# Who copies the key rows of the second score operand: VectorE or GpSimd

## The chip, the cores and the metric

The kernel runs on one core of a Trainium2 chip. The core has a matrix engine (TensorE, PE in the rows, with a queue of its own for weight loads, PEld), a vector engine (VectorE, DVE), a scalar engine (ScalarE, ACT), a general one (GpSimd, POOL) and a queue that issues the transfers (SyncE, SP). The metric is the device time of one execution in microseconds, as the median of several runs. The times of single instructions come from one further execution that was profiled.

## The reference

An attention with a forgetting bias for 8 batches of 8 heads, 576 positions and 64 values a head, and behind it a channel mix of width 512 and 1024:

```
scores = q @ k.T / sqrt(64)
cum = cumsum(max(s, 0))
bias = -(cum[query] - cum[key])
scores = where(causal, -1e9, scores + min(bias, 0))
attn = softmax(scores)
x = attn @ v                              # heads side by side: 8 x 576 x 512
xk = mu_k * x + (1 - mu_k) * x_prev       # x_prev: the position before
xr = mu_r * x + (1 - mu_r) * x_prev
out = sigmoid(xr @ w_r) * (max(xk @ w_k, 0) ** 2 @ w_v)
```

## The kernel before

Every product that must be exact to float32 is split in high and low halves: an operand x becomes xh (x rounded to the matrix engine's format fp32r) and xl = x - xh, and the product is a sum of two or three matmuls.

For the scores of a head (`scores`, matmuls at line 761) there are two passes. The first multiplies G (the rounded queries, both halves of the partitions alike) with KH. KH holds the rounded keys on 64 partitions and their low part on the other 64. The second pass multiplies QL (the low part of the queries on 64 partitions, and three rows of ones) with KL. KL holds the keys on 64 partitions and, below them, three rows with the running sums of s, which bring the bias. The first four visits (the early part of the first batch) use a plain form without these halves.

`split_qk` makes these operands for two heads at a time (j is 0 or 1), from the raw keys k and the raw queries, which lie in buffers called raw: the three rows of sums by a transfer (line 687), ScalarE's copy of the keys into K, which is KH's high half (line 693), GpSimd's subtraction for KH's low half (line 697), VectorE's cast of the keys into KL (line 703), ScalarE's copy of the queries into G (line 708), and GpSimd's subtraction for QL (line 712). It is called 32 times, for 64 heads. KL, QL, G and KH have three buffers each and raw four.

Other names that the prediction uses: line 779 is VectorE's masking of the scores with the running minimum nm; line 797 ScalarE's exponents into W; lines 834 and 839 the sum and its reciprocal rinv (GpSimd, then VectorE); line 813 GpSimd's normalisation of W, five pieces to a head; line 856 the transposes of W on TensorE into the bank t; lines 885 and 889 ph (ScalarE's rounding of the transposed weights) and pl (VectorE's low part); lines 1005 and 1019 the matmuls with V into po; line 632 V's low part on GpSimd, after ScalarE's copy at line 628; lines 1123, 1130, 1152 and 1156 the mixing of neighbouring positions and its halves xh and xl; lines 1184, 1226 and 1251 the matmuls of the channel mix, which works on 18 chunks of 256 positions; line 608 the low half of a weight.

The order of the instructions on every engine is made by a planner in the kernel, the class `Plan`, before the program is built. Each step is added with its engine, an assumed duration and what it reads and writes. The planner lets all engines run by these assumptions, forward and backward in turns, and keeps the best of 20 orders. The functions pe, act, dve, pool and dma add a step to an engine; two of them are:

```python
def dve(emit, reads, writes, n, rate=0.96, extra=70, quarters=(0, 0)):
    return at_quarters(plan.add("DVE", n / rate + extra, emit, reads, writes), quarters)
...
def pool(emit, reads, writes, n, extra, rate=0.8333, quarters=(0, 0)):
    return at_quarters(plan.add("POOL", n * rate + extra, emit, reads, writes), quarters)
```

quarters says on which quarters of the partitions a step reads and writes; the planner puts a gap of 20 ns where they change from a step to the next on an engine. Each engine works through its part of the order strictly in sequence.

Of the kernel before, what the change touches and what calls it, by code (L numbers as in the profile page):

```python
# [29 lines left out]
def f32(ap):  # L30
    return ap.bitcast(F32)
# [281 lines left out]
def forgetting_attention_then_channel_mix(  # L313
# [16 lines left out]
    nc = tc.nc  # L330
# [22 lines left out]
    def sbuf(shape, tag, bufs=1, dtype=F32):  # L353
        return plan.buffer(sb, shape, dtype, tag, bufs)
# [15 lines left out]
    def at_quarters(i, quarters):  # L370
        if quarters != (0, 0):
            plan.quarters[i] = quarters
        return i

    def act(emit, reads, writes, n, extra=51, table=0, quarters=(0, 0)):
        return at_quarters(
            plan.add("ACT", n * 0.8333 + extra, emit, reads, writes, land=table), quarters
# [8 lines that stand above are left out]
    def dma(emit, reads, writes, ns):  # L386
        return plan.add("SP", 1.286 * ns, emit, reads, writes, land=1300)
# [279 lines left out]
    def ahead(emit, what, n):  # L667
        due, plan.due = plan.due, -2.0e5
        dve(emit, [], [what], n)
        plan.due = due  # L670

    def split_qk(b, hp, qs, k):

        nq, nk = qs[0].n, k.n
        found = []
        for j in range(2):
            own, other = slice(64 * j, 64 * j + 64), slice(64 - 64 * j, P - 64 * j)  # L680
            QQ, K = (sbuf([P, n], x, 3, F32R) for n, x in ((nq, "G"), (nk, "KH")))
            QL, KB = (sbuf([P, S], x, 3, F32R) for x in ("QL", "KL"))
            if made[0] < 3:
                made[0] += 1
                ahead(lambda QL=QL: nc.vector.memset(f32(QL.get()[64:67]), 1.0), (QL, 1), S)
            dma(
                lambda j=j, KB=KB: nc.sync.dma_start(
                    f32(KB.get()[64:67, 0:nk]), cum3_d.ap[b * H + 2 * hp + j, :, 0:nk]
                ),
                [(cum3_d, i) for i in range(3)], [(KB, 1)], 40,  # L690
            )
            act(
                lambda own=own, K=K: nc.scalar.copy(K.get()[own], k.get()[own]),  # L693
                [(k, j)], [(K, j)], nk, 90,
            )
            pool(
                lambda own=own, other=other, K=K: nc.gpsimd.tensor_tensor(  # L697
                    out=K.get()[other], in0=k.get()[own], in1=f32(K.get()[own]), op=ALU.subtract
                ),
                [(k, j), (K, j)], [(K, 1 - j)], nk, 210, 2.21, (2 * j, 2 - 2 * j),  # L700
            )
            dve(
                lambda own=own, KB=KB: nc.vector.tensor_copy(KB.get()[0:64, 0:nk], k.get()[own]),  # L703
                [(k, j)], [(KB, 0)], nk, 1.92, 150, (2 * j, 0),
            )
            x = qs[j]
            act(
                lambda x=x, QQ=QQ: nc.scalar.copy(QQ.get(), x.get()),  # L708
                [(x, 0), (x, 1)], [(QQ, 0), (QQ, 1)], nq, 90,
            )  # L710
            pool(
                lambda x=x, QQ=QQ, QL=QL: nc.gpsimd.tensor_tensor(  # L712
                    out=QL.get()[0:64, 0:nq], in0=x.get()[0:64], in1=f32(QQ.get()[0:64]),
                    op=ALU.subtract,
                ),
                [(x, 0), (QQ, 0)], [(QL, 0)], nq, 210, 2.21,
            )
            found.append(((QQ, K, P), (QL, KB, 67)))
        return found
# [632 lines left out]
    def prepare(n):  # L1352
        qs, ks = loaded.pop(n)
        b, hp, tiles = visits[n]
        vn = load_values(b, hp, -(-KN[tiles[-1]] // P), n < PLAIN)
        QKs[n] = [[(x, ks)] for x in qs] if n < PLAINQ else split_qk(b, hp, qs, ks)
        Vs[n] = vn if n < PLAIN else split_v(vn, vn.n // P)
# [119 lines left out]
```

## Time and profile before

| | |
|---|---|
| median of 3 runs | 872.01 us (871.11 to 875.14) |
| the profiled execution | 871.47 us, of it span of the instructions 869.7 us |
| TensorE matmuls busy | 851.7 us, 98% of the span |
| TensorE weight loads busy | 751.0 us, 86% |
| VectorE busy | 698.5 us, 80% |
| ScalarE busy | 688.4 us, 79% |
| GpSimd busy | 449.5 us, 52% |
| granted TensorE clock | 0.999 of full speed |

Busy times are the sum of an engine's instructions without overlaps. Matmuls follow each other in a pipeline, each counted from its start to its modelled end, so a busy TensorE can still be one that starts its matmuls late. The span runs from the first to the last instruction.

### The profile page before, as it was taken

Reading aid. Unit: us, or ns where it says so; the run is one execution under the profiler, and the core shown is the slowest. Engines: PE = TensorE matmul, PEld = TensorE weight load, DVE = VectorE, ACT = ScalarE, POOL = GpSimd, SP = SyncE. Lnnn points to the kernel's source line nnn. Section 1 sums busy time; section 2 is a strip of 40 time slices with the busy share of each in tenths; the row PEclk is TensorE's granted clock in tenths of the full one; section 3 lists DMA queues with packets and bytes.
Section 4 is the critical chain, followed back from the end, with each engine's and each line's share of the span. In section 5 each row is a group of like instructions: output and inputs, shape, how many; then the busy total and the mean of one; then the engine's idle time right before and its main releaser. Section 6 shows DMA issues by size and latency. Waiting matters only on the chain.

```text
span 869.7 us, 17512 instructions
## 1 busy us (share of the span) xinstructions
PE 851.7 (98%) x5519; PEld 751.0 (86%) x5519; DVE 698.5 (80%) x2143; ACT 688.4 (79%) x1854; POOL 449.5 (52%) x719
## 2 busy tenths in 40 slices
PE   9999999999999999999999999999999999999998
PEld 8778789789888888989898988898988889888986
DVE  8999789889888998789878888888888888555431
ACT  6999999999978987898979787988887978445331
POOL 5877887884754665455646545445653642000000
PEclk9999999999999999999999999999999999999999
DMA  8775233251332323223322313132412110100100
GB/s 248 254 233 154 86 115 109 85 153 47 109 117 67 120 64 110 67 83 93 89 88 72 109 55 120 58 104 72 122 55 92 44 62 16 57 22 34 49 25 24
DMA packets 48125, 80.10 MB, mean 92 GB/s; under 512 B 8160, under 2 KB 21472, under 8 KB 48032
## 3 DMA queue, kind: packets, MB, share of 16 engines
q1 hardware_dynamic: 48032, 78.99, 29.7%
q8 instruction: 43, 0.70, 0.3%
q14 instruction: 50, 0.41, 0.2%
HBM read 59.64 MB, written 19.33 MB: 91 GB/s over the span
## 4 chain that ended last, share of the span: by engine, by line
PE 76%; DVE 12%; ACT 8%; issue 3%; DMA 1%; SPq 0%; POOL 0%; ACTq 0%; DVEq 0%
PE m L1251 16%; PE m L1184 16%; PE m L1226 9%; PE s L761 8%; PE po L1019 7%; PE t L856 7%; DVE W L779 3%; ACT W L797 3%; DVE KL L703 2%; DVE pl L889 2%; PE t L1251 2%; PE po L1005 2%; PE s L1184 2%; PE t L1184 2%; PE s L750 1%
## 5 line engine op out<-in xcount | busy, mean ns | idle before, releaser
L1184 PE MATMUL m<-xh,w_k 128*128 128x256 f32 x976 | 205.5, 288 | 0.5 <-ACT xh L1152 0.3
L797 ACT ACTIVATE W<-W,nm 64x64 f32<-64x64 f32 (+4 forms) x320 | 179.6, 562 | 26.3 <-DVE nm L779 22.0
L1251 PE MATMUL m<-w_v,kh 128*128 128x512 f32 x528 | 187.6, 406 | 0.0
L813 POOL TENSOR_SCALAR W<-W,rinv 128x192 f32<-128x192 f32 (+4 forms) x320 | 166.7, 540 | 25.4 <-DVE rinv L839 23.8
L1184 PEld LDWEIGHTS m<-xh,w_k 128*128 128x128 f32 x976 | 160.2, 189 | 3.0 <-ACT xh L1152 0.7
L779 DVE CUSTOM_DVE_ANT_0 W<-s,lower 128x448 f32<-128x448 f32 (+5 forms) x320 | 130.1, 414 | 26.2 <-PE s L761 21.0
L1184 PE MATMUL m<-xl,w_k 128*128 128x256 f32 x488 | 138.9, 285 | 0.0
L856 PE MATMUL t<-ident,W 128*128 128x128 f32 (+1 forms) x736 | 134.0, 275 | 4.5 <-DVE xT L1057 1.8
L697 POOL TENSOR_TENSOR KH<-raw,KH 64x576 fp32r<-64x576 f32 x64 | 92.9, 1451 | 83.9 <-ACT KH L693 45.5
L889 DVE TENSOR_TENSOR pl<-t,ph 128x512 fp32r<-128x512 f32 x224 | 106.4, 484 | 11.9 <-ACT ph L885 9.9
L856 PEld LDWEIGHTS t<-ident,W 128*128 128x128 f32 (+1 forms) x736 | 89.5, 137 | 25.7 <-DVE xT L1057 2.8
L1251 PEld LDWEIGHTS m<-w_v,kh 128*128 128x128 f32 x528 | 97.9, 189 | 14.3 <-ACT g L1238 0.3
L761 PE MATMUL s<-KH,G 128*64 128x64 f32 (+1 forms) x360 | 108.7, 309 | 0.5 <-DVE nm L779 0.5
L885 ACT CAST ph<-t 128x512 fp32r<-128x512 f32 x224 | 93.2, 424 | 17.4 <-PE t L856 14.6
L761 PE MATMUL s<-KL,QL 67*64 67x64 f32 (+1 forms) x360 | 106.1, 299 | 0.0
L1251 PE MATMUL m<-w_v,kl 128*128 128x512 f32 x264 | 106.0, 402 | 0.0
L1130 DVE SCALAR_TENSOR_TENSOR xp<-x,mu,xp 128x256 f32<-128x256 f32 (+3 forms) x184 | 76.3, 415 | 26.5 <-ACT xp L1123 24.1
L1226 PE MATMUL m<-w_r,xh 128*128 128x512 f32 x264 | 95.1, 406 | 0.5 <-DVE kl L1213 0.5
L1123 ACT ACTIVATE xp<-x,mu 128x256 f32<-128x256 f32 (+3 forms) x184 | 77.6, 422 | 22.3 <-DMA x<-x_d 11.7
L712 POOL TENSOR_TENSOR QL<-raw,G 64x576 fp32r<-64x576 f32 (+1 forms) x64 | 86.6, 1353 | 13.3 <-ACT G L708 11.2
L1184 PEld LDWEIGHTS m<-xl,w_k 128*128 128x128 f32 x488 | 92.4, 189 | 0.9
L632 POOL TENSOR_TENSOR V<-vn,V 128x320 fp32r<-128x320 f32 x56 | 48.4, 882 | 70.9 <-ACT V L628 64.5
(161 smaller groups left out, 1899.6 us busy)
## 6 DMA issues: line engine op xcount, KB each, us to landing
raw<-in_q SPq DMA_DIRECT2D x112, 144.0 KB
raw<-in_k SPq DMA_DIRECT2D x32, 288.0 KB
out<-g SPq DMA_DIRECT2D x36, 256.0 KB
vn<-in_v SPq DMA_DIRECT2D x28, 320.0 KB
x_d<-xT SPq DMA_DIRECT2D x28, 288.5 KB
x<-x_d SPq DMA_DIRECT2D x11, 514.0 KB
w_k<-in_moe_w_k SPq DMA_DIRECT2D x8, 512.0 KB
w_v<-in_moe_w_v SPq DMA_DIRECT2D x8, 512.0 KB
```

What stands on the lines that cost most here:

```text
L697: lambda own=own, other=other, K=K: nc.gpsimd.tensor_tensor(out=K.get()[other], in0=k.get()[own], in1=f32(K.get()[own]), op=ALU.subtract),
L712: lambda x=x, QQ=QQ, QL=QL: nc.gpsimd.tensor_tensor(out=QL.get()[0:64, 0:nq], in0=x.get()[0:64], in1=f32(QQ.get()[0:64]), op=ALU.subtract,),
L761: lambda x=x, G=G, K=K, n=n: nc.tensor.matmul(ps.get()[:m, :w], G.get()[:n, q0 : q0 + m], K.get()[:n, k0 : k0 + w], start=x == 0, stop=x == 1,
L779: lambda a=a, e=e, to=to, i=i: nc.vector.tensor_tensor_reduce(out=W.ap[:m, to : to + e - a], in0=ps.get()[:m, a - k0 : e - k0], in1=lower. ...
L797: lambda: nc.scalar.activation(W.ap[:m, :n], W.ap[:m, :n], AF.Exp, bias=nm.get()[:m, 3 * t + mi : 3 * t + mi + 1], scale=-1.0, accum_out=s ...
L813: lambda: nc.gpsimd.tensor_scalar(out=to.ap[:m, c : c + n], in0=W.ap[:m, :n], scalar1=rinv.get()[:m, t : t + 1], scalar2=1.0, op0=ALU.mult ...
L856: lambda: nc.tensor.transpose(ps.get()[0:m, place : place + P], pt[t].ap[:, k0 + front(t, tiles) : k0 + front(t, tiles) + m], ident.ap,),
L885: act(lambda: nc.scalar.copy(strips(ph), src()), [ps], [(ph, k) for k in ks], n * m)
L889: lambda: nc.vector.tensor_tensor(out=strips(pl), in0=src(), in1=f32(strips(ph)), op=ALU.subtract),
L1184: lambda u=u, f=f, c=c, n=n, w=w, x=x: nc.tensor.matmul(ps.get()[:, u * CT : (u + 1) * CT], weight["k", c, f // 4].get()[:, w, f % 4 * P : ...
L1226: lambda c=c, n=n, x=x, w=w: nc.tensor.matmul(ps.get(), x.get()[:, c, ts], weight["r", c, 0].get()[:, w], start=c == 0 and n == 0, stop=c ...
L1251: lambda f=f, n=n, x=x, w=w: nc.tensor.matmul(ps.get(), x.get()[:, f, ts], weight["v", f, 0].get()[:, w], start=f == 0 and n == 0, stop=f ...
```

## The change

The cast of the keys into KL moves from VectorE to GpSimd, with the duration that the planner assumes for GpSimd (576 x 0.8333 + 244). ScalarE's copy of the keys is given the quarters of the partitions on which it works, which no instruction uses, only the planner.

```diff
             act(
                 lambda own=own, K=K: nc.scalar.copy(K.get()[own], k.get()[own]),
-                [(k, j)], [(K, j)], nk, 90,
+                [(k, j)], [(K, j)], nk, 90, quarters=(2 * j, 2 * j),
             )
...
-            dve(
-                lambda own=own, KB=KB: nc.vector.tensor_copy(KB.get()[0:64, 0:nk], k.get()[own]),
-                [(k, j)], [(KB, 0)], nk, 1.92, 150, (2 * j, 0),
+            pool(
+                lambda own=own, KB=KB: nc.gpsimd.tensor_copy(KB.get()[0:64, 0:nk], k.get()[own]),
+                [(k, j)], [(KB, 0)], nk, 244, 0.8333, (2 * j, 0),
             )
```

Both edits change what the planner sees, and it writes a new order for all engines. Two places show what becomes of the instructions. In these rows a name before the arrow is written and those behind it are read; the numbers in the names are those of buffers and differ between the two programs.

The first place is on VectorE, around the 61st of the 64 casts, where VectorE changes from the scores of one head to those of the next (line 779 writes W_72, then W_71). Before, it reads:

```order
L889 TENSOR_TENSOR pl<-t_310,ph_1439 128x512
L779 ISA W_72,nm_254<-s_146,lower,nm_254 128x64
L779 ISA nm_254 128x1
L779 ISA W_71,nm_229<-s_143,lower 64x64
L779 ISA nm_229 64x1
L703 CAST KL_569<-raw_357 64x576
L1156 TENSOR_TENSOR xl_897<-xp_307,xh_882 128x512
L889 TENSOR_TENSOR pl<-t_316,ph_1439 128x384
L889 TENSOR_TENSOR pl<-t_310,ph_1439 128x256
L839 RECIPROCAL rinv_313<-rinv_313 128x5
```

Of the change, VectorE's order has at the same change of heads:

```order
L889 TENSOR_TENSOR pl<-t_291,ph_1416 128x512
L779 ISA W_72,nm_213<-s_151,lower,nm_213 128x64
L779 ISA nm_213 128x1
L779 ISA W_71,nm_181<-s_149,lower 64x64
L779 ISA nm_181 64x1
L889 TENSOR_TENSOR pl<-t_291,ph_1416 128x256
L889 TENSOR_TENSOR pl<-t_296,ph_1416 128x384
L839 RECIPROCAL rinv_271<-rinv_271 128x5
```

The cast is gone, the subtraction for xl stands ten rows ahead of the first of these, and the two pieces of pl have changed places.

The second place is on GpSimd, in the preparation of the pair of heads to which that cast belongs. Before, it reads:

```order
L632 TENSOR_TENSOR V_1411<-vn_100,V_1411 128x5x64 x2
L697 TENSOR_TENSOR KH_524<-raw_357,KH_524 64x576
L1415 MEMSET xT_201 128x1
L712 TENSOR_TENSOR QL_110<-raw_433,G_439 64x576
L834 TENSOR_SCALAR rinv_313<-sums_157 128x5
L726 MEMSET sums_157 128x1
L813 TENSOR_SCALAR W_72<-W_72,rinv_313 128x192
L813 TENSOR_SCALAR W_72<-W_72,rinv_313 128x320
L813 TENSOR_SCALAR W_72<-W_72,rinv_313 128x448
L813 TENSOR_SCALAR W_72<-W_72,rinv_313 64x64
L813 TENSOR_SCALAR W_72<-W_72,rinv_313 128x576
```

Of the change, the same pair of heads reads:

```order
L703 CAST KL_552<-raw_299 64x576
L712 TENSOR_TENSOR QL_109<-raw_381,G_366 64x576
L697 TENSOR_TENSOR KH_468<-raw_299,KH_468 64x576
L632 TENSOR_TENSOR V_1401<-vn_92,V_1401 128x5x64
L834 TENSOR_SCALAR rinv_271<-sums_157 128x5
L632 TENSOR_TENSOR V_1401<-vn_92,V_1401 128x5x64
L813 TENSOR_SCALAR W_72<-W_72,rinv_271 128x192
L813 TENSOR_SCALAR W_72<-W_72,rinv_271 128x320
L813 TENSOR_SCALAR W_72<-W_72,rinv_271 128x448
L813 TENSOR_SCALAR W_72<-W_72,rinv_271 64x64
L813 TENSOR_SCALAR W_72<-W_72,rinv_271 128x576
```

The cast of the head's keys stands ahead of its subtractions, QL's has moved ahead of KH's, and V's two pieces come after them, with the sum of line 834 between. The five normalisations of line 813 keep their places at the end.

## Rows read from the trace of the kernel before

**Rows 1.** Windows: stretch in us, its length, busy us of each engine (instructions), clock, transfers
```profile
0.00:240.00 240.00, 230.46 (x1531) 199.31 (x1532) 218.25 (x638) 221.62 (x618) 184.19 (x298) 1.00 0.47 144
240.00:700.00 460.00, 455.25 (x2986) 405.15 (x2984) 390.43 (x1295) 387.67 (x1055) 252.40 (x394) 1.00 0.28 85
700.00:870.00 170.00, 165.97 (x1005) 146.50 (x1005) 89.86 (x212) 79.11 (x183) 12.91 (x27) 0.99 0.11 37
```
**Rows 2.** The chain that ended last, its shares of the span by engine and line
```profile
by line: PE m L1251 16.2%; PE m L1184 16.1%; PE m L1226 9.4%; PE s L761 8.0%; PE po L1019 6.9%; PE t L856 6.6%; issue 2.7%; DVE W L779 2.6%; ACT W L797 2.6%; DVE KL L703 2.3%; DVE pl L889 2.0%; PE t L1251 1.9%; PE po L1005 1.9%; PE s L1184 
```
**Rows 3.** Line 703: its group (busy us, mean ns, idle before); its durations, shortest, median, longest
```profile
L703 DVE CAST KL<-raw 64x576 fp32r<-64x576 f32 x64 | 50.1, 784 | 1.0
L703 DVE CAST KL<-raw x64: 417/518/2062, 33.5 to 698.3; 64x576 fp32r<-64x576 f32 x64
```
**Rows 4.** Windows of line 703 alone, in the first and the middle stretch
```profile
0.00:240.00 240.00, 20.89 (x26) 1.00 0.47 144
240.00:700.00 460.00, 29.26 (x38) 1.00 0.28 85
```
**Rows 5.** Timeline from 659 to 663 us: start, length, instruction [idle before, releaser]
```profile
659.42 1.43 POOL L712 TENSOR_TENSOR QL<-raw,G 64x576 fp32r<-64x576 f32 x1 [0.57 <-ACT G L708]
...
659.60 1.56 DVE L703 CAST KL<-raw 64x576 fp32r<-64x576 f32 x1
...
661.69 0.87 DVE L889 TENSOR_TENSOR pl<-t,ph 128x384 fp32r<-128x384 f32 x2
...
662.28 0.42 PE L1019 MATMUL po<-pl,V 128*64 128x448 f32 x1 [0.85 <-DVE pl L889]
...
662.75 0.43 POOL L813 TENSOR_SCALAR W<-W,rinv 128x192 f32<-128x192 f32 x1 [1.33 <-DVE rinv L839]
```
**Rows 6.** Timeline from 243.7 to 248 us
```profile
244.02 1.42 POOL L712 TENSOR_TENSOR QL<-raw,G 64x576 fp32r<-64x576 f32 x1 [0.64 <-ACT G L708]
...
244.10 2.06 DVE L703 CAST KL<-raw 64x576 fp32r<-64x576 f32 x1
...
246.67 0.42 PE L1019 MATMUL po<-pl,V 128*64 128x448 f32 x1 [0.81 <-DVE pl L889]
```
**Rows 7.** Waits of TensorE's load queue: us in total, times, longest
```profile
PEld po L1019 <- DVE pl L889: 7.2, 12, 1.3
PEld po L1005 <- ACT ph L885: 3.3, 5, 1.0
PEld t L856 <- DVE xT L1057: 2.8, 4, 0.8
PEld t L856 <- ACT ph L922: 2.5, 6, 0.7
PEld t L856 <- DVE pl L889: 2.4, 11, 0.4
PEld s L761 <- DVE nm L779: 2.0, 6, 0.9
PEld t L856 <- DVE pl L943: 1.7, 2, 0.9
PEld t L1019 <- DVE pl L889: 1.3, 2, 0.7
```
**Rows 8.** Groups on GpSimd that are nearest to the new cast; the fill by its durations
```profile
L697 POOL TENSOR_TENSOR KH<-raw,KH 64x576 fp32r<-64x576 f32 x64 | 92.9, 1451 | 83.9 <-ACT KH L693 45.5 <-PE m L1184 9.0 <-PE s L761 7.9
L813 POOL TENSOR_SCALAR W<-W,rinv 128x576 f32<-128x576 f32 x64 | 48.1, 752 | 0.0
...
L465 POOL MEMSET raw<- x1: 577/577/577, 0.9 to 0.9; 64x576 f32 x1
```
**Rows 9.** Line 1156 on VectorE by its durations
```profile
L1156 DVE TENSOR_TENSOR xl<-xp,xh x72: 640/687/694, 48.7 to 832.8; 128x512 fp32r<-128x512 f32 x72
```
**Rows 10.** Waits of GpSimd
```profile
POOL rinv L834 <- ACT W L797: 70.4, 32, 13.5
POOL V L632 <- ACT V L628: 64.5, 17, 9.5
```

## The prediction

> **What bounds the kernel now.** I read the busy time by stretches first [rows 1]. The program has three stretches: up to 240 us everything runs at once (weight splitting, attention, the first chunks), from 240 to 700 us attention and channel mix alternate, and after 700 us little but channel mix is left. TensorE is busy nearly all the time in each, but its matmuls overlap, so that share says little of how often it waited. The telling numbers are those of its feeders: in the first stretch VectorE is busy 218.25 of 240 us (91%) and ScalarE 221.62 (92%), GpSimd 184.19 (77%); in the middle one VectorE has 390.43 of 460 us (85%), ScalarE 387.67 (84%), GpSimd 252.40 (55%). So VectorE and ScalarE run level just behind TensorE, and GpSimd has room, least of it early.
>
> Next the chain of work that ended last [rows 2]: mostly matmul lines, but the key cast at line 703 alone carries 2.3% of 869.7 us, 20.0 us. That is a lot for 64 instructions. Their own row [rows 3] says why: shortest 417 ns, median 518, mean 784, longest 2062. Something stretches them.
>
> The timeline shows what. At 659.42 us GpSimd starts a 1.43 us subtraction for QL; at 659.60 VectorE starts the cast, which takes 1.56 us, ending 0.31 us after the subtraction. Behind it in VectorE's order, as shown above, stand xl (line 1156) and pl (line 889), which starts at 661.69; the matmul on pl starts at 662.28 after TensorE has stood 0.85 us, "released by pl", and the normalisation on GpSimd (line 813) waits 1.33 us for its reciprocal, which is queued behind pl [rows 5]. At 244.10 us it is the same with 2.06 us of cast and 0.81 us of standing TensorE [rows 6]. Other VectorE work is not stretched so: the 72 subtractions of line 1156 lie between 640 and 694 ns [rows 9].
>
> Last the waits of TensorE's weight-load queue [rows 7]: the six rows that VectorE ends sum to 7.2 + 2.8 + 2.4 + 2.0 + 1.7 + 1.3 = 17.4 us. This and the chain's 20.0 us are two upper views of what VectorE costs TensorE today.
>
> **The change part by part.**
>
> *Removed from VectorE*: 64 casts, 50.1 us [rows 3], of it 20.89 us in the first stretch and 29.26 us in the middle [rows 4]. Taken at the shortest, 64 x 417 ns = 26.7 us is copying; the other 23.4 us is stretching. VectorE falls to 197.4 of 240 us (82%) and 361.2 of 460 us (79%). What reaches TensorE: in the two places looked at, 0.85 + 0.81 = 1.66 us of standing matmuls for 1.56 + 2.06 = 3.62 us of cast, 46% [rows 5, 6]. Lower bound 0 (all waits are taken over by other work), upper bound the 20.0 us of the chain. I take 46% of the 20.0 us: 9.2 us, which is about half of the 17.4 us of visible waits.
>
> *Added to GpSimd*: 64 casts of 64x576. No such row exists. The nearest below is the fill of a tile of the same shape, 577 ns; the nearest above the subtraction with two inputs and the same shape, 1451 ns; between them the one-input multiply of 128x576, 752 ns [rows 8]. One input and one output make it most like the last: 752 ns, 48.1 us in all. In the first stretch that is 26 x 0.752 = 19.6 us, GpSimd 203.8 of 240 us (85%); in the middle 38 x 0.752 = 28.6 us, 281 of 460 us (61%). In the middle it has cover: it stood idle 83.9 us ahead of the KH subtraction (45.5 us of that for ScalarE's K copy) [rows 8], 64.5 us ahead of V's subtraction and 70.4 us ahead of the sum of line 834 [rows 10], and the new cast stands ahead of that KH subtraction in the order. Without cover, queued behind it on GpSimd are the KH and QL subtractions, and then the five normalisations of a head, for which the transposes of line 856 wait. Lower bound of the harm 0, upper bound the 19.6 us of the crowded first stretch. I charge 1 us, close to the lower end, since 55.8 us of that stretch are idle on GpSimd.
>
> *The wait moves with the cast.* It needs the raw keys alone, which the subtraction on the same queue needs too, so no new transfer is waited for. The raw keys had three readers on three engines (ScalarE's copy, the subtraction, the cast) and now have two of them on GpSimd; I cost that at nothing because a reader on GpSimd, the subtraction, already held the buffer before, and 207.6 us of the middle stretch are idle there [rows 1] to cover a later release. Without that cover the next load into raw would come late by one cast, 752 ns.
>
> *The quarters given to ScalarE's copy* add no instruction; they and the moved task only change what the planner assumes. It then writes another order for every engine. The orders shown above are alike in kind (VectorE's loses the cast row, the rest keeps its sequence but for neighbours), so I count this at zero, with 4 us to either side for the luck of a new order.
>
> Sum: 871.47 (the profiled execution) - 9.2 + 1 = 863.3, say 863.5 us. The profiled execution lies 0.5 us below the median 872.01 of the runs, so nothing is added for that. It is 1.0% faster.
>
> One rule speaks against it. The Trainium skill, "Perfetto Trace Analysis", section "Optimizing Scalar/DVE Operations", warns that moving work between VectorE and GpSimd might not help, because they share a pair of SBUF ports which a two-port VectorE instruction holds alone. The trace agrees with the sharing, and shows it from the other side: the cast was stretched to 1.56 us by a GpSimd instruction [rows 5]. By that rule the sum would be 871.5; it is the third rival. I go by the rows, since they show one VectorE line that is stretched, and it is the one that leaves.
>
> **The rivals.**
>
> 1. *All of the chain's share comes back* (VectorE no longer late anywhere, also for the reciprocal and the normalisation behind it): 871.5 - 20.0 = 851.5 us. For it: the casts' delay is unplanned, and the order is static, so each delay travels on. Against it: in both places other VectorE work stood between the cast and pl, and TensorE lost under half.
>
> 2. *ScalarE takes over*. It is already the busier one in the first stretch [rows 1], and TensorE's load queue waits for it too, 3.3 us and 2.5 us in two rows beside those counted above [rows 7]. If VectorE is early and ScalarE late, a quarter of the 9.2 us may be left: 871.5 - 2.3 + 1 = 870.2 us.
>
> 3. *The two engines go on hindering each other*, now with GpSimd's cast: the time saved on VectorE is lost in its other instructions, 871.5 us. Against it stand the narrow times of line 1156 [rows 9].
>
> 4. *Slower: GpSimd becomes late in the first stretch.* If a cast there cost as much as the two-input subtraction, 1.451 us, 26 of them are 37.7 us, and GpSimd stands at 221.9 of 240 us, as full as ScalarE. The normalisations then come late by a cast, and with the same 46% reaching TensorE that costs 26 x 1.451 x 0.46 = 17.4 us, against a gain in the middle stretch of 9.2 x 29.26/50.15 = 5.4 us: 871.5 + 17.4 - 5.4 = 883.5 us. It decides from a cast of about (221.6 - 184.2)/26 = 1.44 us on. For it: GpSimd is at 77% there before the change. Against it: the one-input row is half of that.
>
> **How the numbers follow.** My forecast has 0.60 (863.5, itself 859 to 867 by the 4 us of the order), the whole share 0.08 (851.5), ScalarE 0.15 (870.2), mutual hindrance 0.05 (871.5), slower 0.12 (883.5). A measurement of this kernel tells about 0.5%, 4.4 us, from no change, so faster is below 867.6: 0.60 + 0.08 = 0.68; same 0.15 + 0.05 = 0.20; slower 0.12. The range leaves out the slower rival and most of the first: 854 to 871.5 us.
>
> **What would show it.** Right: line 703 stands on GpSimd at 0.65 to 0.9 us with hardly any scatter; VectorE's total falls by about 50 us; the chain holds next to nothing of line 703; the load queue's waits that VectorE ends fall from 17.4 to about half; GpSimd's busy time rises by about 48 us, and it releases few TensorE waits. Wrong: new waits of line 856 for line 813 in the first 240 us (rival 4), waits for ScalarE's ph, V or exponents of the size of those that went (rival 2), VectorE lines longer than before (rival 3), or a start or an end of the program that the new order moved, which none of these terms holds.

## The result, and the profile after

| | before | after |
|---|---|---|
| median | 872.14 us (4 runs, 871.11 to 875.14) | 861.17 us (4 runs, 858.65 to 864.47) |
| profiled execution | 871.47 us | 858.65 us |

The ratio is 0.987 with a 95% interval of 0.983 to 0.991: 11.0 us less, where the forecast of 863.5 us was 8.6 us less than this median. The rows below are of the profiled execution, 12.8 us faster than that of before; it was the fastest of its four, so they show 1.8 us more than the medians do.

The page of the kernel after: its span, the busy times, the chain by engine, and the group of line 703.

```profile
span 856.9 us, 17457 instructions
...
PE 846.0 (99%) x5492; PEld 751.4 (88%) x5492; DVE 654.0 (76%) x2079; ACT 687.6 (80%) x1854; POOL 485.7 (57%) x783
...
PE 91%; ACT 4%; DVE 2%; DMA 1%; issue 1%; POOL 0%; ACTq 0%; DVEq 0%; POOLq 0%
...
L703 POOL CAST KL<-raw 64x576 fp32r<-64x576 f32 x64 | 42.4, 662 | 88.7 <-PE s L761 55.4
```

The 64 casts are on GpSimd, 662 ns each; VectorE has 654.0 us to do instead of 698.5. The chain of work that ended last is now 91% TensorE, and VectorE has 2% of it. The chain by line no longer has line 703 near the top, where it had 2.3% [rows 2]:

```profile
by line: PE m L1251 21.4%; PE m L1184 18.6%; PE s L761 10.0%; PE m L1226 9.8%; PE po L1019 8.9%; PE t L856 8.7%; PE t L1251 2.0%; PE po L1005 1.9%; PE t L1184 1.7%; PE s L1184 1.7%; PE s L750 1.2%; PE s L739 1.1%; PE t L1019 1.0%; PE t L956
```

The windows of the same three stretches as in [rows 1]:

```profile
0.00:240.00 240.00, 233.82 (x1534) 204.01 (x1535) 205.56 (x626) 225.53 (x631) 201.60 (x331) 0.99 0.49 148
240.00:700.00 460.00, 459.02 (x3026) 411.95 (x3025) 368.36 (x1278) 391.74 (x1070) 276.53 (x439) 1.00 0.28 84
700.00:870.00 170.00, 153.13 (x936) 135.43 (x934) 80.03 (x178) 70.30 (x155) 7.57 (x16) 0.99 0.10 34
```

VectorE is busy 205.56 of the first 240 us (it was 218.25), GpSimd 201.60 (184.19). After 700 us 936 matmuls are left where 1005 were: 69 of them have moved ahead. In the first stretch 3 more matmuls are started, but 71 of those of before were fillers of line 399, which keep TensorE busy before there is work, and 44 of those of after are. So 30 of the 69 were gained in the first stretch and 40 in the middle one (3026 against 2986), within a record or two.

The waits of TensorE's load queue that answer to [rows 7]:

```profile
PEld t L856 <- ACT ph L922: 2.6, 4, 1.1
PEld s L761 <- DVE nm L779: 2.4, 10, 0.6
PEld t L856 <- ACT ph L885: 2.3, 4, 0.8
...
PEld po L1005 <- ACT ph L885: 1.8, 4, 1.0
PEld t L856 <- DVE pl L889: 1.4, 5, 0.4
...
PEld t L856 <- DVE xT L1057: 0.4, 2, 0.2
...
PEld po L1019 <- DVE pl L889: 0.3, 1, 0.3
...
PEld t L1019 <- DVE pl L889: 0.2, 1, 0.2
```

Those that VectorE ends sum to 2.4 + 1.4 + 0.4 + 0.3 + 0.2 = 4.7 us, from 17.4; the longest row of before, on pl, went from 7.2 to 0.3. Of ScalarE's two rows there, one went from 3.3 to 1.8 us, the other from 2.5 to 2.6; all rows of the view that ScalarE ends sum to 9.5 us, from 10.7.

At the place of [rows 5], the same change of heads, the timeline now reads:

```profile
650.22 0.22 DVE L779 CUSTOM_DVE_ANT_0 W<-s,lower 64x64 f32<-64x64 f32 x1 [1.60 <-POOL V L632]
...
650.37 0.88 DVE L889 TENSOR_TENSOR pl<-t,ph 128x256 fp32r<-128x256 f32 x2
...
651.38 0.37 PE L1019 MATMUL po<-pl,V 128*64 128x448 f32 x1
```

VectorE has done its earlier work and stands idle for 1.60 us before it masks the next scores; the two pieces of pl follow at once, and the matmul on pl at 651.38 starts without a wait. Before, TensorE had stood 0.85 us there.

### The profile page after: what moved, and what is told of

Same layout as the page of the kernel before. It is cut to its first block, busy times and chain, and to the rows that moved or that the text cites. A ratio compares the mean times of both kernels' runs of the same rounds, so it can differ in the third digit from the quotient of the medians.

```text
span 856.9 us, 17457 instructions
## 1 busy us (share of the span) xinstructions
PE 846.0 (99%) x5492; PEld 751.4 (88%) x5492; DVE 654.0 (76%) x2079; ACT 687.6 (80%) x1854; POOL 485.7 (57%) x783
## 4 chain that ended last, share of the span: by engine, by line
PE 91%; ACT 4%; DVE 2%; DMA 1%; issue 1%; POOL 0%; ACTq 0%; DVEq 0%; POOLq 0%
PE m L1251 21%; PE m L1184 19%; PE s L761 10%; PE m L1226 10%; PE po L1019 9%; PE t L856 9%; PE t L1251 2%; PE po L1005 2%; PE t L1184 2%; PE s L1184 2%; PE s L750 1%; PE s L739 1%; PE t L1019 1%; PE t L956 1%; ACT W L797 1%
## 5 line engine op out<-in xcount | busy, mean ns | idle before, releaser
L797 ACT ACTIVATE W<-W,nm 128x320 f32<-128x320 f32 (+4 forms) x320 | 179.4, 562 | 19.1 <-DVE nm L779 16.1
L813 POOL TENSOR_SCALAR W<-W,rinv 128x448 f32<-128x448 f32 (+4 forms) x320 | 165.4, 535 | 27.1 <-DVE rinv L839 25.9
L779 DVE CUSTOM_DVE_ANT_0 W<-s,lower 64x64 f32<-64x64 f32 (+5 forms) x320 | 130.0, 414 | 33.9 <-PE s L761 24.3
L1251 PEld LDWEIGHTS m<-w_v,kh 128*128 128x128 f32 x528 | 97.7, 189 | 15.2 <-DVE r L600 0.3
L761 PE MATMUL s<-KH,G 128*64 128x64 f32 (+2 forms) x360 | 108.5, 313 | 0.2 <-DVE nm L779 0.2
L761 PE MATMUL s<-KL,QL 67*64 67x64 f32 (+2 forms) x360 | 107.4, 302 | 0.0
L697 POOL TENSOR_TENSOR KH<-raw,KH 64x576 fp32r<-64x576 f32 x64 | 91.3, 1426 | 17.0 <-ACT KH L693 13.6
L703 POOL CAST KL<-raw 64x576 fp32r<-64x576 f32 x64 | 42.4, 662 | 88.7 <-PE s L761 55.4
```

The source lines that it names most:

```text
L697: lambda own=own, other=other, K=K: nc.gpsimd.tensor_tensor(out=K.get()[other], in0=k.get()[own], in1=f32(K.get()[own]), op=ALU.subtract),
L761: lambda x=x, G=G, K=K, n=n: nc.tensor.matmul(ps.get()[:m, :w], G.get()[:n, q0 : q0 + m], K.get()[:n, k0 : k0 + w], start=x == 0, stop=x == 1,
L779: lambda a=a, e=e, to=to, i=i: nc.vector.tensor_tensor_reduce(out=W.ap[:m, to : to + e - a], in0=ps.get()[:m, a - k0 : e - k0], in1=lower. ...
L797: lambda: nc.scalar.activation(W.ap[:m, :n], W.ap[:m, :n], AF.Exp, bias=nm.get()[:m, 3 * t + mi : 3 * t + mi + 1], scale=-1.0, accum_out=s ...
L813: lambda: nc.gpsimd.tensor_scalar(out=to.ap[:m, c : c + n], in0=W.ap[:m, :n], scalar1=rinv.get()[:m, t : t + 1], scalar2=1.0, op0=ALU.mult ...
L1251: lambda f=f, n=n, x=x, w=w: nc.tensor.matmul(ps.get(), x.get()[:, f, ts], weight["v", f, 0].get()[:, w], start=f == 0 and n == 0, stop=f ...
```

## The experiments

Each ratio is to the kernel before, timed beside it on the same chip; "less than before" is meant so too. Differences between two changed kernels are of medians taken partly at different times. "Order of before" means that the planner is told what it was told before, so that all other instructions stand as they stood.

**The cast alone is moved, the order stays.**

```diff
             dve(
-                lambda own=own, KB=KB: nc.vector.tensor_copy(...),
+                lambda own=own, KB=KB: nc.gpsimd.tensor_copy(...),
                 [(k, j)], [(KB, 0)], nk, 1.92, 150, (2 * j, 0),
```

> The planner still takes the cast for a VectorE step of 450 ns, so the order of all other instructions is that of before; the cast alone is issued on GpSimd, at its old place in the order. My theory (VectorE is relieved of a cast that GpSimd stretches): most of the gain is here, 861 to 865 us. Rival, the new order makes the gain: 870 to 874 us. Rival, GpSimd gets late where nobody planned the cast: 866 us or more, with new waits of the normalisation.

Measured: 863.82 us, ratio 0.990 (0.987 to 0.992), 7.8 us less. So most of the gain comes without a new order. Three of the waits of its load queue:

```profile
PEld t L856 <- POOL W L813: 2.4, 5, 1.0
PEld t L856 <- DVE pl L889: 2.2, 10, 0.6
...
PEld po L1019 <- DVE pl L889: 0.8, 3, 0.3
```

The wait of po for VectorE's late pl has nearly gone, from 7.2 us [rows 7] to 0.8; that of the transposes for pl has not, 2.2 us from 2.4. And there is a new wait for the normalisation on GpSimd, 2.4 us: the price of a cast that the plan did not have there. With the planned order of the change the load queue has no wait for line 813.

**The new order, the cast back on VectorE.**

```diff
             pool(
-                lambda own=own, KB=KB: nc.gpsimd.tensor_copy(...),
+                lambda own=own, KB=KB: nc.vector.tensor_copy(...),
                 [(k, j)], [(KB, 0)], nk, 244, 0.8333, (2 * j, 0),
```

> The reverse: the order of the change (the planner takes the cast for a GpSimd step), but the cast is issued on VectorE. My theory: the gain is gone, 868 to 876 us, and the casts scatter from 0.42 to 2 us again. Rival, the new order makes the gain: 860 to 864 us.

Measured: 878.94 us, ratio 1.008 (1.005 to 1.010), so the new order brings no gain while VectorE keeps the cast. It is not the order alone that is tested here, for it was made for a VectorE without the cast. Its casts by group, and three waits of the load queue:

```profile
L703 DVE CAST KL<-raw 64x576 fp32r<-64x576 f32 x64 | 40.0, 625 | 1.0
```

```profile
PEld s L761 <- DVE nm L779: 5.2, 14, 1.4
PEld t L856 <- DVE pl L889: 4.1, 12, 0.6
...
PEld t L1019 <- DVE pl L889: 2.7, 3, 1.5
```

The casts are stretched less than before (625 ns in the mean against 784), and yet TensorE waits no less for VectorE: the three rows shown grew from 2.0, 2.4 and 1.3 us [rows 7], that of po for pl fell from 7.2 to 2.2, and all that VectorE ends sum to 21.6 us, from 19.6. I put the 7.3 us of loss down to an order that has left VectorE no time for the casts; that is argued and not shown.

**The cast stays on VectorE, as a reduction.** The reduction runs over an axis of length 1, so it copies.

```diff
-nc.vector.tensor_copy(KB.get()[0:64, 0:nk], k.get()[own])
+nc.vector.tensor_reduce(
+    out=KB.get()[0:64, 0:nk],
+    in_=k.get()[own].rearrange("p (n o) -> p n o", o=1),
+    axis=mybir.AxisListType.X, op=ALU.max,
+)
```

> The order of before, and the cast stays on VectorE, but in another form: a reduction over an axis of length 1, which copies element by element. I expect about 0.65 us each without scatter, 42 us in all, where the casts had 50.1. If it is the stretching (casts that run late by up to 1.6 us at places that nobody planned) that costs, most of the gain is here too: 862 to 866 us. If it is the load of VectorE, hardly anything: 869 to 872 us.

Measured: 864.70 us, ratio 0.991 (0.988 to 0.993), 6.9 us less. Its group and its durations:

```profile
L703 DVE TENSOR_REDUCE KL<-raw 64x576 fp32r<-64x576 f32 x64 | 47.5, 742 | 1.0
```

```profile
L703 DVE TENSOR_REDUCE KL<-raw x64: 705/746/751, 34.5 to 691.7; 64x576 fp32r<-64x576 f32 x64
```

VectorE spends 47.5 us on it, nearly the 50.1 us of before, in the order of before. What differs is that no instance takes longer than 751 ns, where 2062 ns were reached [rows 3]. GpSimd's subtraction for KH, which took up to 1708 ns before, takes at most 1443 ns here. So it was the stretching, of the casts and of GpSimd's instructions beside them, that cost most, and not a load of this size; which of the two the stretching hurt more, this run does not separate.

**Only the quarters of ScalarE's copy.**

```diff
-                [(k, j)], [(K, j)], nk, 90,
+                [(k, j)], [(K, j)], nk, 90, quarters=(2 * j, 2 * j),
```

> Only the second edit: ScalarE's copy is given its quarters, the cast stays on VectorE; the planner writes a new order. My theory: nothing but the luck of an order, 868 to 876 us. Rival, the quarters are what brings the gain: about 861 us.

Measured: 875.33 us, ratio 1.004 (1.002 to 1.005). The second edit alone does not help; its order is 3.7 us slower.

**The reduction, planned.** The planner is told `nk, 0.96, 70` instead of `nk, 1.92, 150`.

> The element-by-element form on VectorE again, now with the planner told its duration (576/0.96 + 70 ns = 670), so that a new order is written. If the load of VectorE costs nothing once it is planned, this reaches the change: 858 to 864 us. If the freed 50 us of VectorE are worth something of their own, it stays at the 864.7 us of the old order or above: 864 to 870 us.

Measured: 862.38 us, ratio 0.990 (0.988 to 0.991). With all of the keys still copied by VectorE this is 1 us from the change.

**The change without the quarters.** The second edit is undone, the cast stays on GpSimd.

> The change without its second edit, ScalarE's quarters; the planner writes another new order with the cast on GpSimd. I expect 859 to 866 us: the cast on GpSimd brings the gain and the order decides within 3 us. Rival: the quarters carry 3 us or more of it, 865 us or above.

Measured: 867.73 us, ratio 0.996 (0.995 to 0.997), 6.6 us slower than the change: outside what I expected, and on the rival's side. Windows of this run, and then of the change: the first 120 us, and pieces of 2 us around the stretches at half clock.

```profile
0.00:120.00 120.00, 111.52 (x683) 92.69 (x684) 96.09 (x260) 103.66 (x286) 97.38 (x164) 0.97 0.61 185
52.00:54.00 2.00, 0.51 (x4) 0.21 (x2) 1.28 (x3) 1.98 (x6) 1.83 (x3) 0.98 0.89 229
54.00:56.00 2.00, 1.76 (x7) 1.64 (x8) 1.96 (x7) 1.97 (x6) 1.61 (x3) 0.50 0.91 353
94.00:96.00 2.00, 1.57 (x6) 1.02 (x7) 1.70 (x7) 2.00 (x6) 2.00 (x3) 0.72 0.00 0
96.00:98.00 2.00, 2.00 (x8) 1.66 (x7) 1.11 (x3) 2.00 (x6) 1.89 (x2) 0.50 0.03 5
```

```profile
0.00:120.00 120.00, 114.09 (x715) 96.70 (x715) 101.32 (x276) 108.35 (x299) 100.14 (x169) 0.99 0.62 186
44.00:46.00 2.00, 0.40 (x2) 0.21 (x2) 2.00 (x6) 2.00 (x9) 0.85 (x2) 1.00 0.49 100
46.00:48.00 2.00, 2.00 (x7) 1.73 (x8) 1.75 (x6) 2.00 (x6) 1.96 (x3) 0.59 0.91 362
```

In 120 us this order starts 683 matmuls, 51 of them fillers; the change starts 715, 44 of them fillers. So 39 real ones are missing already, and 60 more are left after 700 us (996 against 936): most of the loss is made early. There the granted clock falls to 0.50 of full speed (1.2 of 2.4 GHz) twice, after 54 and from 94 us on, and in the change once, after 46 us, to 0.59 in the mean of 2 us. Before two of the three TensorE had been busy for only 0.51 and 0.40 of 2 us. The clock does not explain the 6.6 us, though. Of the eight executions of this kernel four had a mean granted clock of 1.000 and took 866.93 to 867.23 us; the four with 0.995 to 0.997 took 868.22 to 870.38, and the profiled one, at 869.67, is of these. The four of the change had 0.996 to 0.998 and took 858.65 to 864.47.

**The cast issued twice on GpSimd**, in the order of the change.

```diff
-lambda own=own, KB=KB: nc.gpsimd.tensor_copy(KB.get()[0:64, 0:nk], k.get()[own]),
+lambda own=own, KB=KB: [nc.gpsimd.tensor_copy(KB.get()[0:64, 0:nk], k.get()[own]) for _ in range(2)],
```

> The change with each cast issued twice on GpSimd, in the same order: 64 more instructions of 0.66 us, 42 us more on GpSimd, 18 us of it in the first stretch, so a cast costs 1.32 us, a little under the 1.44 us from which I had expected GpSimd to become late. If GpSimd has the room: 861 to 865 us. If the extra time reaches TensorE at 46% in the first stretch: 861 + 27 x 0.66 x 0.46 = 869 us; at 46% everywhere 880 us.

Measured: 869.36 us, ratio 0.995 (0.993 to 0.998), 8.2 us more than the change. Its windows, and the load queue's waits that GpSimd ends:

```profile
0.00:240.00 240.00, 229.93 (x1471) 197.75 (x1472) 196.93 (x599) 217.32 (x604) 208.60 (x343) 0.99 0.47 142
240.00:700.00 460.00, 458.72 (x3027) 411.43 (x3026) 368.27 (x1273) 393.31 (x1072) 307.55 (x483) 1.00 0.29 86
```

```profile
PEld t L856 <- POOL W L813: 3.8, 8, 1.2
...
PEld s L761 <- POOL QL L712: 1.6, 1, 1.6
```

1471 matmuls are started in the first 240 us, 63 fewer than in the change; in the middle 3027, as many as there (3026). So in the middle, where GpSimd is busy 307.55 of 460 us, the second cast is free. But not all that is lost in the first stretch is its doing. The fillers of line 399, of the change and then of this run:

```profile
L399 PE MATMUL po<-ident x44: 243/260/368, 1.9 to 25.7; 128*128 128x192 bf16 x44
```

```profile
L399 PE MATMUL po<-ident x44: 242/367/383, 1.9 to 29.9; 128*128 128x192 bf16 x44
```

Both programs have the same order, and each begins with fillers of 367 ns. In the change they take about 250 ns from 5.5 us on. In this execution the last of 367 ns starts at 8.3 us, and the next filler, of 246 ns, only at 15.2 us; up to 13.7 us its first matmuls at line 750 take up to 881 ns, where none of that line takes over 516 in the change. The granted clock is given as 1.00 in both. Up to 20 us it has started 97 matmuls, the change 127, and it reaches its first cast on GpSimd at 37.9 us, the change at 33.7. So 4.2 of the 10.9 us between the two profiled executions (869.58 and 858.65) were lost before GpSimd had run any cast. In the 13 other profiled executions the slow start ends by 8 us; why it lasted longer here is open. The five executions fall in two groups, 864.54 and 865.44, and 869.36 to 870.19; only the one of 869.58 was profiled. My estimate of what the second cast costs is therefore 4 to 7 us: 3.8 us from the change's median to the mean of the faster two, 6.7 us from the profiled pair less 4.2.

**The reduction issued twice on VectorE**, in the order of before.

```diff
-lambda own=own, KB=KB: nc.vector.tensor_copy(KB.get()[0:64, 0:nk], k.get()[own]),
+lambda own=own, KB=KB: [nc.vector.tensor_reduce(...) for _ in range(2)],
```

> The order of before and the element-by-element form on VectorE, issued twice: 64 more instructions of 0.74 us, 47 us more on VectorE, all of them alike and none planned. At the 46% of my prediction this costs 22 us over the single form: 887 us. If VectorE's time costs only where a cast is very late (over 1 us), 868 to 875 us.

Measured: 906.27 us, ratio 1.040 (1.038 to 1.042), 41.6 us more than with one. For 64 x 0.742 = 47.5 us more on VectorE that is 88%, nearly twice the share that I had taken. The waits of the load queue (the edit makes line 889 line 894, 779 line 784, 1057 line 1062):

```profile
PEld t L861 <- DVE pl L894: 10.7, 21, 1.1
PEld po L1024 <- DVE pl L894: 9.6, 13, 1.3
PEld s L766 <- DVE nm L784: 9.3, 16, 1.5
PEld t L861 <- DVE xT L1062: 7.8, 8, 2.0
```

**The true price told to the planner.** GpSimd's cast takes 662 ns, so the planner is told `nk, 182` instead of `nk, 244`; once with and once without the quarters.

> The change with the planner told the 662 ns that the cast takes on GpSimd, instead of 724; a new order. If the 62 ns matter, better than the change, 857 to 860 us; if an order is luck, anywhere from 859 to 868 us, the span between the change (861) and the run without quarters (868).

> The same without ScalarE's quarters. If the quarters have a worth of their own (ScalarE's changes of partitions cost time that the planner should know), this is some 6 us slower than its twin with them, as the change without quarters was: 866 to 870 us. If that difference was the luck of one order, 859 to 868 us and no fixed sign.

Measured: 861.85 us with the quarters, ratio 0.988 (0.986 to 0.991), and 865.80 us without, ratio 0.992 (0.990 to 0.994). The price makes no clear difference: 0.7 us more than the change with the quarters, 1.9 us less than its twin without. The quarters again go with the faster order.

**The reduction at its true price**, `nk, 0.96, 142`, 742 ns.

> The element-by-element form on VectorE, the planner told its 742 ns instead of 670. VectorE has its old load, planned and without scatter: 860 to 865 us, as with 670 ns. If VectorE's load has a price of its own that the old plan hid, a dearer step makes it show: 865 us or above.

Measured: 863.47 us, ratio 0.990 (0.988 to 0.992).

**The cast of before at its mean.** The planner is told `nk, 1.92, 484`, 784 ns.

> The cast on VectorE as before, the planner told 784 ns, its measured mean, instead of 450. If all that hurt before was a plan that was wrong on the mean, this gains: 862 to 867 us. If it is the scatter (most near 0.45, some near 2 us) and what the cast holds up on GpSimd, no plan with one number mends it: 868 to 876 us.

Measured: 867.83 us, ratio 0.994 (0.992 to 0.997), 4.0 us less than before. The durations of its casts, and the longest one:

```profile
L703 DVE CAST KL<-raw x64: 441/456/3024, 29.3 to 690.7; 64x576 fp32r<-64x576 f32 x64
```

```profile
104.46 2.17 POOL L813 TENSOR_SCALAR W<-W,rinv 128x320 f32<-128x320 f32 x4
...
105.17 3.02 DVE L703 CAST KL<-raw 64x576 fp32r<-64x576 f32 x1
...
106.60 1.28 POOL L608 TENSOR_TENSOR w_v<-x,w_v 128x512 fp32r<-128x512 f32 x1
...
107.85 1.62 POOL L712 TENSOR_TENSOR QL<-raw,G 64x576 fp32r<-64x576 f32 x1
```

The reduction that is planned at nearly the same length brings 4.4 us more (863.47), though it costs VectorE about as much (742 ns each, where these casts have 794). This fits a plan that is right on the mean and brings a part, with the rest in the scatter and in what the cast holds up on GpSimd. It does not show it: each of the two has an order of its own, and 4 us is what a new order alone has moved here.

No version beat the change clearly; the change with the true price (861.85) is equal to it.

## Why the prediction was right, point by point

*The cast was stretched by GpSimd's instructions, and this reached TensorE.* Shown: with nearly the same load on VectorE and the same order, the form that is not stretched saves 6.9 us. The timeline of the kernel before bears it out for all 64 casts, and not only for the two of [rows 5] and [rows 6]: 33 took over 500 ns, each of these started while a GpSimd instruction ran, and 32 ended 0.31 or 0.32 us after the end of one, the other 0.39 us after. The remaining 31 took at most 474 ns. The Trainium skill, "SBUF — State Buffer", section "Who interferes with whom", says that VectorE's copies and casts between SBUF tensors can use both of VectorE's port pairs, one of them shared with GpSimd, that then whichever of the two engines came first blocks the other, and that a reduction on this chip cannot. The runs agree: the cast scatters from 417 to 2062 ns, the reduction from 705 to 751. GpSimd gains too. Its subtraction for KH, in the program before and then after:

```profile
L697 POOL TENSOR_TENSOR KH<-raw,KH x64: 1405/1428/1708, 32.6 to 695.2; 64x576 fp32r<-64x576 f32 x64
```

```profile
L697 POOL TENSOR_TENSOR KH<-raw,KH x64: 1406/1427/1443, 30.4 to 682.1; 64x576 fp32r<-64x576 f32 x64
```

The longest falls from 1708 to 1443 ns: the cast had held GpSimd up as well.

*46% of the chain's 20.0 us, 9.2 us, less 1 us on GpSimd.* The cast alone moved in the old order gave 7.8 us; the sum said 8.2. As a size it was right. The reason behind it was coarse, and that the size came out so close is in part luck: the 46% came from two places that were looked at because TensorE stood there, and it was taken of the chain's share in proportion. The runs show no proportion. One copy of 742 ns on VectorE costs 0.9 us in all against none there (864.70 and 863.82, the second with GpSimd's new wait in it), though the old order had kept only 450 ns for it, so that it runs over by 18.7 us in all. A second one, for which no time was kept, costs 41.6 us, 88% of itself. The casts put back on VectorE in the order of the change, for which no time was kept either, cost 17.8 us against the change for 40.0 us, 44%. So the price rises with what VectorE already has to do beyond its plan, and no run here gives a rule for it.

*GpSimd's cast at 752 ns, 48.1 us.* It took 662 ns, 42.4 us, between the bounds and nearer to the lower.

*Cover on GpSimd, 1 us.* No run measures it alone. The load queue's waits that GpSimd ends sum to 1.9 us in the change, from 2.5 before, so with a planned cast the harm is small, as charged; with the cast unplanned in the old order they are 6.3 us. The rows of its idle time show where it went: GpSimd's waits after the change are

```profile
POOL KL L703 <- PE s L761: 55.4, 24, 5.9
POOL rinv L834 <- ACT W L797: 53.4, 31, 11.3
...
POOL V L632 <- ACT V L628: 23.8, 12, 2.9
...
POOL KH L697 <- ACT KH L693: 13.6, 18, 2.2
```

V's wait for ScalarE falls from 64.5 to 23.8 us, the sum's from 70.4 to 53.4 [rows 10], and KH's for its K copy from 45.5 [rows 8] to 13.6; the cast now waits 55.4 us itself, for matmuls of the scores. I had written that the cast needs the raw keys alone. That was wrong: it also needs a free KL buffer, which the score matmuls of three heads before release, and what stands behind it on GpSimd waits with it. It was covered by the same idle time.

*The order, zero with 4 us to either side.* It gave perhaps 3.2 us of the gain: 11.0 us with the new order, 7.8 us with the old. That is not clear of the noise, for the four executions of the change lie between 858.65 and 864.47 us, with the old order's 863.82 inside. The 4 us held: the four planned orders with the cast on GpSimd lie from 2.7 us below to 3.9 us above the old order with the cast there, and the new order of the quarters alone lies 3.7 us above before. Two new orders can so differ by 6.6 us.

*The rivals.* The whole share of the chain did not come back. ScalarE did not take over: its two waits of [rows 7] sum to 4.4 us, from 5.8. The two engines did not go on hindering each other: line 1156 takes 642 to 693 ns after the change, 640 to 694 before [rows 9], and GpSimd's new cast 654 to 671. The load queue's waits for VectorE fell further than to the half that was forecast, from 17.4 to 4.7 us. GpSimd becoming late in the first stretch is real at twice the price, 1.32 us a head, but smaller than the median of that run says: my estimate is 4 to 7 us, all of it in the first stretch. That the 869 us worked out from 46% met the 869.36 us measured is in part luck, since the slow start of 4.2 us is in the measured time.

*What stays open.* Whether the quarters are worth something. With the cast on GpSimd the order with them was faster twice, by 6.6 and 4.0 us; with the cast on VectorE it was slower by 3.7 us. Three pairs of orders do not tell a worth from luck. How the gain divides between casts that are no longer stretched and GpSimd instructions that are no longer held up was not separated. And why the first 120 us of one order run at half clock longer than those of another was not tried.

## What to carry to other kernels

Look at the spread of an instruction's durations and not at its mean alone: one line whose longest is four times its median may be a line that another engine stops, which the timeline beside it shows, and it can do harm in an order that was planned on the short time. Such a line need not move; a slower form that is not stopped brought nearly as much as moving it. And when work moves between engines under a planner, run the move in the old order and the old place in the new order too, for a new order by itself moved the time from 2.7 us down to 3.9 us up here. Last, look at the start of the profiled execution before its stretches are compared with another's: one here had lost 4.2 us before the change could act.

## What the runs showed of the hardware that was not expected

A stretched cast does not always get its turn between two instructions of GpSimd that follow close on each other. The 3.02 us above, from 105.17 us on, span the last three of the four normalisations shown (line 813), a weight's low half of 1.28 us (line 608) and the start of the subtraction behind it: the cast ended at 108.19, 0.31 us after the low half, when that next instruction was already on GpSimd's record. So it was passed over at three changes of instruction and got its turn at the fourth. In the kernel before, a waiting cast met 15 such changes (the next instruction, fills left out, on record before the last had ended) and got its turn at 8 of them. One of these reads:

```profile
465.62 1.43 POOL L712 TENSOR_TENSOR QL<-raw,G 64x576 fp32r<-64x576 f32 x1
...
466.83 0.54 DVE L703 CAST KL<-raw 64x576 fp32r<-64x576 f32 x1
...
467.03 1.76 POOL L813 TENSOR_SCALAR W<-W,rinv 128x192 f32<-128x192 f32 x3
```

Here the cast ends at 467.37, 0.32 us after the subtraction's end, with the normalisation already on record. The Trainium skill says in the same section that the other engine fully blocks while the first has the shared pair for its instruction. The trace agrees where the cast got its turn at once; where it was passed over, up to three times, it was blocked for longer than that sentence says, and what decides between the two no run here shows.

TensorE's first matmuls are slow in every profiled execution. The fillers of 128x192 take 367 ns and then 246. In 13 of the 14 executions the last slow one starts by 7.6 us; in one, the cast issued twice on GpSimd, matmuls were slow up to 13.7 us, while the granted clock was given as 1.00.

A cast of 64x576 from one SBUF tensor to another takes GpSimd 654 to 671 ns, less than its multiply of 128x576 by a scalar of each partition (752 ns), and is as steady as VectorE's reduction, 705 to 751 ns.
